# One 128-byte pad and one moved sum in a layer-norm, attention and Mish kernel

## The chip, the core and the metric

The kernel runs on one core of a Trainium2 chip. The core has TensorE for matrix products (PE in the profile, with its weight loads listed apart as PEld), VectorE (DVE), ScalarE (ACT) and GpSimd (POOL) for elementwise work, and SyncE (SP), which here issues all the DMAs. The metric is the device time of one execution in microseconds. Three executions of the kernel before took 1108.43, 1108.59 and 1108.93 us; their median is 1108.59 us.

## What is computed

All data are float32: x is 2048 x 576, and the result is the sum of x, a sliding attention and a two-layer Mish network, both on the layer-normed x. Cut to what matters:

```python
xn = layernorm(x)                                   # over the 576 columns, no scale or shift
qkv = xn @ wqkv                                     # 32 heads of 18 columns
# each position looks at itself and 7 earlier ones, 2 apart; positions before the start are masked
attn = softmax(q . k[pos - 2 * (0..7)] * 18 ** -0.5)
A = (attn-weighted sum of v) @ wo
h = xn @ w1 + b1                                    # 4608 columns
B = (h * tanh(softplus(h))) @ w2                    # Mish, then back to 576 columns
out = x + A + B
```

## The kernel before, in words

**Tiles and halves.** The 2048 tokens are worked in two halves (`hf` 0 and 1) of 1024, each half in two groups of 512 (`TB`). For each group the normed, transposed x is one tile `xt`, with a high part (rounded to the matmul format `F32R`) and a low part (the remainder), since every product is done as three products of high and low parts. The 4608 hidden columns are 18 blocks `q` of 256 (`NP`). Each block runs two steps: `m1_part` (line 738) makes the hidden activations, parts 0 to 5, and `m2_pair`, `m2_cols` or `p_item` multiply them with `w2`. Both steps use Strassen-like sums of quarters (`S` of x, `t` of the weights, `S1` to `S4` of activations), so that seven products do the work of eight.

**Weights of a block.** Block `i` of `w1` becomes four tiles: `wa`, `wc`, `t0` and `t1`. `wc` is the third block of the diff's title: 128 partitions x 2 (high, low) x 384 floats. Function `home` (line 204) gives a tile's tag and number of buffers, and `new` (line 217) allocates it. Tiles of one tag share its buffers and take them in turn, and a buffer is as large as the largest tile of the tag. Tag `wc` has 2 buffers. It also holds some weights of the first stage (`wq`, 2 x 432 floats, 3456 bytes in a partition), so that its two buffers are 3456 bytes each. All other large tiles follow or precede them in one pool. In the first half a block's tiles are made from raw loads, and kept in DRAM; in the second half they are fetched from there. The order of blocks in the second half is 1 to 17 and then 0 (`Q1`, line 33).

A product of `m1_part` has the weights as the stationary operand (128 columns at a time) and `xt` or `S` as the moving one. `wc` is used in part 3 (two matmuls of line 686) and part 5 (six of line 680 and two of line 686), ten matmuls of 512 columns for a block and half.

**The items of the second half.** In the second half, blocks 0 to 7 in the order of that half are taken two at a time (`e` = 0 to 3) into seven products each, `p_item(e, k)` (line 860), in the order `ORD`. An item runs four groups of six matmuls (line 872), each into a PSUM bank of tag `out`, of which there are four, and each followed by one addition into an SBUF accumulator: on DVE at line 878, or for some items a copy on ACT at line 876. So the next item's matmuls need the four additions of the item before. An item's left operand is an activation or a sum of activations: `u_sum` (line 807) makes the sum in place, `u_high` (line 817) its high part on ACT, `u_low` (line 822) its low part on DVE or POOL. Activations come from `mish` (line 716): ACT copies an intermediate product out of PSUM (line 714), DVE adds the next product to it (line 725), and ACT applies Mish (line 726).

**The order of work.** The order is written by hand. `plan` is a list of slots, one for each piece of matmul work; a slot has its own functions, a list of background functions (`before(i, fn)`, line 1164, appends to it), and an estimate of its time. The loop at line 1566 issues, for each slot: what the last slot left as `soon`, the background functions, what was `held` (the run of `mish` from the slot before), the slot's own functions, and then `tail`. Every engine runs its instructions in that order. Attention is cut into steps that are placed as background (`attention`, line 512): POOL multiplies (lines 539 and 577), DVE reduces (lines 544 and 583). For a few slots, among them that of item (0, 4), the set `behind_adds` (line 1495) has the pending reduction issued from `tail`, behind the slot's additions.

The moved sum is `u_sum(0, 6, 1)`: `S4` = `A12` - `S2` of the second block of pair 0, 128 x 512 floats, on DVE. Its slot is two items ahead, that of item (0, 4); before, it is a background function there, ahead of the item's four additions in DVE's order. The same sum for the first block, `u_sum(0, 6, 0)`, is on POOL and stays.

Of the kernel before, what the change touches and what calls it, by code (L numbers as in the profile page):

```python
# [9 lines left out]
F32R = mybir.dt.float32r  # L10
# [7 lines left out]
P = 128  # L18
# [21 lines left out]
def block_kernel(ctx: ExitStack, tc: tile.TileContext, x, wq, wo, w1, b1, w2, mask, out):  # L40
# [4 lines left out]
    sb = ctx.enter_context(tc.tile_pool(name="sb", bufs=2))  # L45
# [158 lines left out]
    def home(kind, i):  # L204
        if kind == "wq":
            g, k = divmod(i, 5)
            tag, bufs = (("wb", 3) if k < 3 else ("wc", 2)) if g % 2 == 0 else (("a0", 3) if k < 3 else ("a1", 2))
            return tag, bufs, 432
        if kind == "wa":
            return f"wa{(i + 1) % 2}", 1, 5 * P  # L210
        if kind == "wc":
            return "wc", 2, 3 * P
        if kind == "w2":
            return "w2", 4, D
        return "wb", 3, 4 * P

    def new(kind, hf, i):
        tag, bufs, width = home(kind, i)
        return sb.tile([P, 2, width], F32R, tag=tag, bufs=bufs, name=f"{kind}_{hf}_{i}")

    def load(kind, i):
# [20 lines left out]
    def make(kind, i):  # L242
        load({"wa": "w1", "wc": "w1", "t0": "w1", "t1": "w1"}.get(kind, kind), i)
        width = home(kind, i)[2]
        if kind == "wa":
            src = loaded["w1", i][0]
        elif kind == "wc":
            src = loaded["w1", i][1][:, 2 * P:5 * P]
        elif kind in ("t0", "t1"):
            src = sums[i][int(kind[1])]  # L250
        else:
            src = loaded[kind, i][:, 0:width]
        t = done[kind, 0, i] = new(kind, 0, i)
        nc.scalar.copy(t[:, 0, :], src)
        low[kind, i] = lambda: nc.vector.tensor_tensor(out=t[:, 1, :], in0=src, in1=t[:, 0, :].bitcast(F32),
                                                       op=ALU.subtract)
# [18 lines left out]
    def fetch(kind, i):  # L275
        w = i
        if kind == "w2":
            w = 2 * Q1[i // 2] + i % 2
        elif kind != "wq":
            w = Q1[i]  # L280
        t = done[kind, 1, i] = new(kind, 1, w)
        nc.sync.dma_start(t.rearrange("p h c -> p (h c)").bitcast(F32), kept[kind, w])
# [509 lines left out]
    def rslotof(q, x):  # L792
        k = q, int(x[1]) - 1, int(x[2]) - 1
        assert owner[where[k]] == k, (k, owner[where[k]])
        return rawact[k]

    def u_src(q, name):
        x = SLOT.get(name, name)
        assert held_.get((q, x)) == name, (q, name, held_.get((q, x)))
        return rslotof(q, x)  # L800
# [6 lines left out]
    def u_sum(e, k, qq):  # L807
        name, q = LEFT[ORD[k]], 2 * e + qq
        eng = nc.gpsimd if (name, qq) in (("S1", 1), ("S4", 0)) else nc.vector
        x, y, op = dict(S3=("A11", "A21", ALU.subtract), S2=("A22", "S3", ALU.subtract), S1=("A11", "S2", ALU.add),  # L810
                        S4=("A12", "S2", ALU.subtract)).get(name, (None,) * 3)
        if x:
            t = rslotof(q, SLOT[name])
            eng.tensor_tensor(out=t, in0=u_src(q, x), in1=u_src(q, y), op=op)
            held_[q, SLOT[name]] = name
# [21 lines left out]
    def p_fetch(e, k):  # L837
        name = RIGHT[ORD[k]]
        t = pw[e, k] = sb.tile([P, 2, 2, HC], F32R, tag="w2", bufs=4, name=f"pw_{e}_{k}")
        nc.sync.dma_start(t.bitcast(F32), kept[name, e])  # L840
# [314 lines left out]
    plan = []  # L1155
# [8 lines left out]
    def before(i, fn):  # L1164
        plan[max(i, 0)][1].append(fn)
# [24 lines left out]
    def first_cast(k, eng):  # L1190
        t = done["wq", 0, k] = new("wq", 0, k)
        nc.scalar.copy(t[:, 0, :], rq0[k])
        return lambda: eng.tensor_tensor(out=t[:, 1, :], in0=rq0[k], in1=t[:, 0, :].bitcast(F32),
                                         op=ALU.subtract)
# [161 lines left out]
    def spot(hf, q, i):  # L1356
        return at["s", hf, q, i]

    for q in range(NP):
        if q == 0:  # L1360
            i = at["q", 0, 3, 1, 0]
            ps_ = dict(raw=i - 3, sums=i - 1, wa=i, wc=i + 1, t0=i + 2, t1=i + 4)
        elif q == 1:
            i = at["q", 0, 3, 0, 0]
# [16 lines left out]
    for q in range(1, 2 * OC + 1):  # L1381
        i = spot(0, q, (3,2)[q > 1])
# [5 lines left out]
    i = spot(0, NP - 1, 0)  # L1388
# [5 lines left out]
    i = at["q", 1, 0, 1, 1]  # L1394
# [4 lines left out]
    i = spot(0, 9, 4)  # L1399
    for k in range(2):  # L1400
        for n, steps in enumerate((
# [4 lines left out]
            for kind, name in steps:  # L1406
                f = dict(l=z_load, s=z_sum, h=z_high, o=z_low, k=z_keep)[kind]
                d = 30 + 2 * n + (n >= 14) if k else 2 * n if n < 10 else (19, 20, 22, 23, 25, 26, 27)[n - 10]
                before(i + d, lambda f=f, name=name, k=k: f(name, k))
    for q in range(NP):  # L1410
        if q == 0:
            i = at["z", JB - 1, 0]
            ps_ = dict(wa=i - 7, t0=i - 6, t1=i - 5, wc=i - 4)
        elif q == 1:
            i = spot(1, 0, 0)
# [9 lines left out]
    for g, (e, k, s) in enumerate(items):  # L1425
        lead = items[g - 3][2] if g >= 3 else spot(1, 0, 5) + 2 * g
        before(lead + 1, lambda e=e, k=k: p_fetch(e, k))
        for qq in range(2):
            ds = {(0, 0): (-6, -5, -5), (0, 1): (-2, -1, -1), (1, 0): (0, -4, -2), (1, 1): (0, -2, -2), (2, 0): (0, -3, -2), (2, 1): (0, -3, -2), (3, 0): (-4, -3, -2), (3, 1): (-4, -2, -1), (4, 0): (0, -3, -3), (4, 1): (0, -3, -2), (5, 0): (-1, -3, -3), (5, 1): (0, -3, -2), (6, 0): (-4, -3, -1), (6, 1): (-4, -3, -2)}[k, qq]
            if e in (1, OC - 1) and (k, qq) == (0, 0):  # L1430
                ds = (-5, -4, -4)
            if e == 0 and k in (3, 5):
                ds = (-3, -2, -1) if k == 3 else (1,) + ds[1:]
            for d, f in zip(ds[1:], (u_high, u_low)):
                before(s + d, lambda f=f, e=e, k=k, qq=qq: f(e, k, qq))
            s2 = items[7 * e + (0 if k == 5 else k)][2] + ds[0]
            before(s2, lambda e=e, k=k, qq=qq: u_sum(e, k, qq))
    J = 2 * OC + 1
    for b in range(NB):
        for j in range(2):  # L1440
# [8 lines left out]
    i = at["q", 0, 1, 1, 0]  # L1449
# [3 lines left out]
    i = at["q", 0, 3, 1, 0]  # L1453
# [5 lines left out]
    i = at["q", 1, 0, 1, 1]  # L1459
    for n in range(8):  # L1460
        c, k = divmod(n, 4)
# [7 lines left out]
    for n in range(0, JB, 2):  # L1469
        i = at["q", 0, 1, 0, n]  # L1470
# [4 lines left out]
    for n in range(TJ):  # L1475
        i = spot(0, 2 + n, 2)
# [3 lines left out]
    i = spot(0, NP - 2, 0)  # L1480
# [7 lines left out]
    for n, (name, pr) in enumerate((name, pr) for name in ("P4", "P5", "P2", "P3") for pr in range(2)):  # L1488
        i = items[dict(P4=0, P5=2, P3=2, P2=3)[name]][2] + pr
# [26 lines left out]
    k = marks[0] - 1  # L1516
    for n in range(steps - len(last_steps)):
        t = 6.111 * n
        k = next(k for k in range(k + 1, len(plan)) if T[k + 1] > t and ok[k])
# [16 lines left out]
    i = spot(1, *(11,3))  # L1536
# [4 lines left out]
    for n, name in enumerate(("T3", "T1", "T2", "T4", "B11", "B21", "B22", "R", "D")):  # L1541
        k = i + 10 + (2, 5, 10, 15, 20, 25, 30, 35, 40)[n]
# [5 lines left out]
    i = spot(1, NP - 1, 0)  # L1548
# [71 lines left out]
```

## Time and profile before

| what | value |
|---|---|
| executions before | 1108.43, 1108.59, 1108.93 us |
| the profiled execution's own time | 1109.51 us |
| its span, first to last instruction | 1107.7 us |
| granted clock | 0.999 |
| busy: PE, PEld | 1100.8 us (99%), 1015.3 us (92%) |
| busy: DVE, POOL, ACT | 850.6 us (77%), 791.1 us (71%), 499.1 us (45%) |
| DMA | 271.60 MB, mean 245 GB/s |

The profiled execution is 0.9 us above the median of the three, and 1.8 us of its time lie outside its span. A share of busy time is a mean over stages; a matmul's end is modelled, so the times from start to start of successive matmuls say more than their durations.

### The profile page before, as it was taken

To read this page: it belongs to the slowest core of one execution; us is meant where nothing else is said; L and a number is where in the kernel's file an instruction comes from. 1 tells how busy PE (TensorE), PEld (TensorE's weight loads), DVE (VectorE), ACT (ScalarE), POOL (GpSimd) and SP (SyncE) were. 2 spreads that over 40 slices of the span, in tenths; PEclk is the share of its full clock that TensorE was granted. 3 is DMA by queue.
4 is the path that set the end of the run, shared out by engine and by line. 5 is a ranking of instruction groups with operands and counts; after the bars stand their busy time and mean duration, and the time that the engine had idled before them with its cause. 6 is when DMAs were issued, how large, how long until landed. Compare 5 with 4: busy or idle time off the path is not lost.

```text
span 1107.7 us, 18208 instructions
## 1 busy us (share of the span) xinstructions
PE 1100.8 (99%) x6550; PEld 1015.3 (92%) x6550; DVE 850.6 (77%) x1367; ACT 499.1 (45%) x917; POOL 791.1 (71%) x639
## 2 busy tenths in 40 slices
PE   9999999999999999999999999999999999999998
PEld 8999899999999999999999888989999999999998
DVE  6368788888889888898656567777876677777786
ACT  5544655544544544545333354434433344343353
POOL 2479777776779688685789667567698976867542
PEclk9999999999999999999999999999999999999999
DMA  6899696868777768676598799656674657776674
GB/s 203 284 311 308 235 343 232 282 239 266 254 259 249 266 222 296 238 263 214 170 323 268 237 358 317 223 192 208 221 222 173 210 195 224 243 288 218 179 234 140
DMA packets 178270, 271.60 MB, mean 245 GB/s; under 512 B 53218, under 2 KB 120068, under 8 KB 178180
## 3 DMA queue, kind: packets, MB, share of 16 engines
q1 hardware_dynamic: 178180, 270.44, 72.0%
q8 instruction: 52, 0.85, 0.3%
q14 instruction: 38, 0.31, 0.1%
HBM read 160.39 MB, written 110.00 MB: 244 GB/s over the span
## 4 chain that ended last, share of the span: by engine, by line
PE 94%; DMA 2%; DVE 2%; ACT 1%; POOL 1%; issue 0%; SPq 0%; DVEq 0%; POOLq 0%
PE h L680 29%; PE po L780 21%; PE po L893 11%; PE pq L348 11%; PE po L872 6%; PE h L686 6%; PE o L1076 5%; PE z L446 4%; DMA t<-kept_t 1%; DMA accP<-in_x 1%; POOL act L732 0%; PE ta L75 0%; DMA acc<-in_x 0%; DVE st L112 0%; DVE u L826 0%
## 5 line engine op out<-in xcount | busy, mean ns | idle before, releaser
L780 PEld LDWEIGHTS po<-w,act 128*128 128x128 f32 x1728 | 236.4, 188 | 6.0 <-POOL act L732 0.4
L780 PE MATMUL po<-w,act 128*128 128x288 f32 x1728 | 240.7, 295 | 0.1
L539 POOL TENSOR_TENSOR pr<-q,kv 128x576 f32<-128x576 f32 x128 | 198.2, 1574 | 9.3 <-DMA q<-q_d 6.1
L732 POOL TENSOR_TENSOR act<-c,act 128x512 fp32r<-128x512 f32 x81 | 107.4, 1326 | 128.1 <-ACT act L731 127.3
L577 POOL TENSOR_TENSOR pv<-L,kv 128x576 f32<-128x576 f32 x128 | 178.1, 1485 | 26.3 <-DVE L L570 21.4
L784 DVE TENSOR_TENSOR acc<-po,acc 128x288 f32<-128x288 f32 x288 | 119.3, 449 | 29.7 <-PE po L780 28.9
L348 PE MATMUL pq<-wq,xt 128*128 128x432 f32 x672 | 136.3, 361 | 0.9 <-ACT xt L81 0.6
L893 PEld LDWEIGHTS po<-w,act 128*128 128x128 f32 x960 | 130.9, 188 | 2.9
L893 PE MATMUL po<-w,act 128*128 128x288 f32 x960 | 132.9, 294 | 0.0
L348 PEld LDWEIGHTS pq<-wq,xt 128*128 128x128 f32 x672 | 125.1, 188 | 7.7 <-ACT xt L81 1.3
L726 ACT ACTIVATE c<-c,b1c 128x512 f32<-128x512 f32 x81 | 58.7, 725 | 138.1 <-DVE c L725 137.8
L680 PE MATMUL h<-xt,t 128*128 128x512 f32 x432 | 110.7, 391 | 0.1
L680 PE MATMUL h<-S,t 128*128 128x512 f32 x432 | 110.5, 391 | 0.0
L583 DVE TENSOR_REDUCE og<-pv 128x144 f32<-128x1152 f32 x64 | 85.9, 1345 | 24.1 <-POOL pv L577 23.9
L680 PE MATMUL h<-xt,wa 128*128 128x512 f32 x432 | 104.1, 390 | 0.0
L714 ACT COPY c<-h 128x512 f32<-128x512 f32 x81 | 47.4, 586 | 124.1 <-PE h L686 73.1
L544 DVE TENSOR_REDUCE L<-pr 128x64 f32<-128x1152 f32 x64 | 85.8, 1342 | 20.9 <-POOL pr L539 20.8
L680 PEld LDWEIGHTS h<-xt,wa 128*128 128x128 f32 x432 | 80.9, 188 | 17.0
L872 PEld LDWEIGHTS po<-pw,u 128*128 128x128 f32 x672 | 92.1, 188 | 3.5 <-DVE accP L878 1.2
L872 PE MATMUL po<-pw,u 128*128 128x288 f32 x672 | 93.8, 295 | 0.8 <-DVE accP L878 0.8
L680 PEld LDWEIGHTS h<-xt,t 128*128 128x128 f32 x432 | 79.1, 188 | 15.1 <-DVE rt L725 0.5
L896 DVE TENSOR_TENSOR accP<-po,accP 128x288 f32<-128x288 f32 x160 | 69.0, 452 | 30.2 <-PE po L893 29.4
(228 smaller groups left out, 1854.3 us busy)
## 6 DMA issues: line engine op xcount, KB each, us to landing
kv<-kv_d SPq DMA_DIRECT2D x64, 396.0 KB, 5.2
kept_t<-t SPq DMA_DIRECT2D x36, 512.0 KB, 4.4
t<-kept_t SPq DMA_DIRECT2D x36, 512.0 KB, 6.5
rw<-in_w SPq DMA_DIRECT2D x36, 320.0 KB, 4.5
kept_wa<-wa SPq DMA_DIRECT2D x18, 640.0 KB, 4.9
kept_w<-w SPq DMA_DIRECT2D x20, 576.0 KB, 4.1
wa<-kept_wa SPq DMA_DIRECT2D x18, 640.0 KB, 5.2
w<-kept_w SPq DMA_DIRECT2D x20, 576.0 KB, 4.3
```

Of the source, the lines that this page charges most:

```text
L348: nc.tensor.matmul(pq[:, 0:432], XT[:, xi, tok], wt[wi][:, hl, 0:432], start=i == 0, stop=i == len(seq) - 1)
L539: nc.gpsimd.tensor_tensor(out=pr[:, x:x + hh], in0=q[:, j0 + x:j0 + x + hh, None, :].to_broadcast([P, hh, W, CU]), in1=win(kt, 0, CU, j0 + ...
L544: nc.vector.tensor_reduce(L[:, k, j0:j0 + hj].rearrange("p j w h -> p (j w h)"), pr.rearrange("p j w (h d) -> p (j w h) d", h=2), axis=AX, ...
L577: nc.gpsimd.tensor_tensor(out=pr[:, x:x + hj].rearrange("p j d w -> p j w d"), in0=L[:, k, x:x + hj, :, h:h + 1].to_broadcast([P, hj, W, DH]),
L583: nc.vector.tensor_reduce(og[:, c0:c0 + DH, :].rearrange("p d j -> p j d"), pr, axis=AX, op=ALU.add)
L680: nc.tensor.matmul(ph, wt[:, wl, wk * P:(wk + 1) * P], X[:, xs, :], start=first and i == 0, stop=last and i == len(seq) - 1, skip_group_ch ...
L732: nc.gpsimd.tensor_tensor(out=a[:, 1, :], in0=t, in1=a[:, 0, :].bitcast(F32), op=ALU.subtract)
L780: nc.tensor.matmul(po, acts[hf, q, b, j][:, al, tok], done["w2", hf, 2 * q + j][:, wl, c * HC:(c + 1) * HC], start=i == 0, stop=i == 5)
L784: nc.vector.tensor_tensor(out=t, in0=po, in1=t, op=ALU.add)
L872: nc.tensor.matmul(po, units[e, k, qq][:, al, tok], w[:, qq, wl, :], start=i == 0, stop=i == 5)
L893: nc.tensor.matmul(po, acts[hf, q, b, j][:, al, tok], done["w2", hf, 2 * q + j][:, wl, c * HC:(c + 1) * HC], start=i == 0, stop=i == 5)
L896: nc.vector.tensor_tensor(out=t, in0=po, in1=t, op=ALU.add)
```

## The change

There are two edits. A tile of tag `wc` made by `new` is allocated as 128 x 896 floats (3584 bytes in a partition, 14 x 256) and cut to its old shape by a view; the buffers of the tag grow from 3456 to 3584 bytes, so that the second lies 128 bytes farther on, and all tiles behind the two 256 bytes farther. And the sum `u_sum(0, 6, 1)` is appended to its slot's own functions, behind `p_item(0, 4)`, where it was a background function of the slot.

```diff
     def new(kind, hf, i):
         tag, bufs, width = home(kind, i)
+        if tag == "wc":
+            return sb.tile([P, 7 * P], F32R, tag=tag, bufs=bufs, name=f"{kind}_{hf}_{i}")[:, 0:2 * width].rearrange(
+                "p (h c) -> p h c", h=2)
         return sb.tile([P, 2, width], F32R, tag=tag, bufs=bufs, name=f"{kind}_{hf}_{i}")
...
             s2 = items[7 * e + (0 if k == 5 else k)][2] + ds[0]
-            before(s2, lambda e=e, k=k, qq=qq: u_sum(e, k, qq))
+            plan[s2][0 if (e, k, qq) == (0, 6, 1) else 1].append(lambda e=e, k=k, qq=qq: u_sum(e, k, qq))
```

## The prediction, made before the result was known

> **What bounds the kernel now.** I read the page first: the span, the busy shares and the chain of work that ended last.
>
> ```profile
> span 1107.7 us, 18208 instructions
> ...
> PE 1100.8 (99%) x6550; PEld 1015.3 (92%) x6550; DVE 850.6 (77%) x1367; ACT 499.1 (45%) x917; POOL 791.1 (71%) x639
> ...
> PE 94%; DMA 2%; DVE 2%; ACT 1%; POOL 1%; issue 0%; SPq 0%; DVEq 0%; POOLq 0%
> ```
>
> PE is busy in 1100.8 of 1107.7 us and carries 94% of the chain. So there are only two ways to gain: to take away one of PE's few waits, or to make matmuls follow each other faster. The two edits aim at one of each. The list of PE's waits comes next:
>
> ```profile
> PE warm L65 <- POOL ident masks.py:199: 1.3, 1, 1.3
> PE po L872 <- DVE accP L878: 0.8, 1, 0.8
> ```
>
> The list has five rows; the other three are single waits of 0.6 us and less for the first normed x and the first weights, in the start. After that there is one wait: an item's matmuls (L872) wait once, 0.8 us, for the additions of the item before (DVE L878). Then the costs of matmuls by group, since PE is otherwise never idle:
>
> ```profile
> L680 PE MATMUL h<-xt,t 128*128 128x512 f32 x432 | 110.7, 391 | 0.1
> ...
> L680 PE MATMUL h<-xt,wa 128*128 128x512 f32 x432 | 104.1, 390 | 0.0
> ...
> L680 PE MATMUL h<-S,wc 128*128 128x512 f32 x216 | 55.8, 393 | 0.0
> L686 PE MATMUL h<-xt,wc 128*128 128x512 f32 x144 | 45.0, 394 | 0.0
> ```
>
> All these have 512 moving columns and 128 stationary ones. With `t` or `wa` as weights the mean is 390 to 391 ns, with `wc` 393 to 394. The third block's tile is the odd one out, and the change pads its buffers.
>
> **The padding.** It adds no instruction, no wait and no DMA, and moves none in any queue, SP's included; the bytes of each load and store stay 2 x 384 floats a partition. What changes is addresses. A buffer of 3456 bytes is 13.5 x 256, so now the two buffers of the tag differ by half of 256 bytes in where they start; at 3584 bytes they agree. Tiles take the buffers in turn, so odd blocks have the second and even blocks the first, in both halves (in the second half one `R2` tile takes the first buffer ahead of block 1). If the address matters, odd and even blocks must differ. I look at the timeline of PE for the same pair of matmuls (part 3) in successive blocks 9, 10, 11 of the first half, and 13, 14, 15 of the second:
>
> ```profile
> 321.44 0.64 PE L686 MATMUL h<-xt,wc 128*128 128x512 f32 x2
> ...
> 345.59 0.62 PE L686 MATMUL h<-xt,wc 128*128 128x512 f32 x2
> ...
> 369.67 0.64 PE L686 MATMUL h<-xt,wc 128*128 128x512 f32 x2
> ...
> 906.18 0.64 PE L686 MATMUL h<-xt,wc 128*128 128x512 f32 x2
> ...
> 930.35 0.62 PE L686 MATMUL h<-xt,wc 128*128 128x512 f32 x2
> ...
> 954.44 0.64 PE L686 MATMUL h<-xt,wc 128*128 128x512 f32 x2
> ```
>
> The pair shows 0.64 us in odd blocks and 0.62 in even ones. A whole block, which holds the same matmuls each time, takes 345.59 - 321.44 = 24.15 us from an odd block's pair to the next, and 369.67 - 345.59 = 24.08 from an even one's: 0.07 more with the second buffer. In the second half it is 24.17 against 24.09, 0.08 more. For the early blocks of the second half, where items lie between, I compare block 5 with block 6, from the start of a run to the start of what follows it:
>
> ```profile
> 709.83 0.64 PE L686 MATMUL h<-xt,wc 128*128 128x512 f32 x2
> 710.32 0.97 PE L872 MATMUL po<-pw,u 128*128 128x288 f32 x6
> ...
> 718.54 1.55 PE L680 MATMUL h<-S,wc 128*128 128x512 f32 x6
> ...
> 720.40 1.78 PE L680 MATMUL h<-xt,wa 128*128 128x512 f32 x7
> ...
> 730.88 0.62 PE L686 MATMUL h<-xt,wc 128*128 128x512 f32 x2
> 731.34 0.83 PE L872 MATMUL po<-pw,u 128*128 128x288 f32 x5
> ...
> 739.56 1.53 PE L680 MATMUL h<-S,wc 128*128 128x512 f32 x6
> ...
> 741.37 1.98 PE L680 MATMUL h<-xt,wa 128*128 128x512 f32 x8
> ```
>
> Part 3's pair: 0.49 against 0.46 us. Part 5's eight (six of L680 and two of L686 behind them): 720.40 - 718.54 = 1.86 against 741.37 - 739.56 = 1.81. Together 0.08. I take 0.07 for the nine odd blocks of the first half and 0.08 for the nine of the second: 0.63 + 0.72 = 1.35, rounded to **-1.4 us** since the matmuls next to the runs show a few ns too. The rows are rounded to 0.01, which on a difference of two stretches is worth 0.02 a block, 0.4 in all: the bounds are -1.0 and -1.8. None of it needs cover: PE is the bound and takes it directly, unless a later wait eats it (a rival below).
>
> The Trainium skill speaks against this edit: "SBUF — State Buffer", section "Who interferes with whom", says that PE never waits on another engine's SBUF access, and names only VectorE's and GpSimd's shared ports as a place of contention; it knows no cost of a matmul's operand address. By that page the edit is worth 0 and the sum would be 1108.6. The trace disagrees with 24.15 against 24.08 us, and I go by the trace.
>
> **The moved sum.** Around PE's 0.8 us wait the timeline of all engines reads:
>
> ```profile
> 683.03 1.74 POOL L814 TENSOR_TENSOR ra<-ra,rm 128x512 f32<-128x512 f32 x1
> 683.55 1.77 DVE L814 TENSOR_TENSOR rm<-rm,rm 128x512 f32<-128x512 f32 x1
> ...
> 684.73 7.04 POOL L539 TENSOR_TENSOR pr<-q,kv 128x576 f32<-128x576 f32 x4
> ...
> 685.24 1.54 DVE L878 TENSOR_TENSOR accP<-po,accP 128x288 f32<-128x288 f32 x4
> 685.43 0.62 ACT L820 CAST u<-rm 128x512 fp32r<-128x512 f32 x1
> ...
> 685.74 3.47 PE L872 MATMUL po<-pw,u 128*128 128x288 f32 x24 [0.81 <-DVE accP L878]
> 685.95 0.58 ACT L714 COPY rt<-h 128x512 f32<-128x512 f32 x1
> 686.70 1.34 DVE L544 TENSOR_REDUCE L<-pr 128x64 f32<-128x1152 f32 x1
> 687.96 0.68 DVE L826 TENSOR_TENSOR u<-rm,u 128x512 fp32r<-128x512 f32 x1
> 688.56 0.68 DVE L725 TENSOR_TENSOR rt<-h,rt 128x512 f32<-128x512 f32 x1
> ...
> 689.29 1.23 PEld L680 LDWEIGHTS h<-xt,t 128*128 128x128 f32 x6 [0.32 <-DVE rt L725]
> ```
>
> The moved sum is the DVE row at 683.55, 1.77 us. Behind it stand the four additions (685.24), and PE waits 0.81 us for them. With the sum behind them the additions start at 683.55 and end at 685.09, the first bank is free at about 684.0, and PE goes on without the wait, at 685.74 - 0.81 = 684.93. So far the edit gains 0.81.
>
> What is late next? The item's 24 matmuls would end 0.81 earlier, at 688.40 instead of 689.21. The next matmul (689.29, part 4) accumulates into the bank that DVE's addition L725 reads, and starts 0.05 after that addition's end at 689.24; the weight-load row names it as releaser. So the wait moves there, unless that addition is earlier as well. DVE works without a pause from 683.55 to 689.24, and the move only permutes its order, so the addition is earlier only if the sum gets shorter. Its price here:
>
> ```profile
> L814 DVE TENSOR_TENSOR rm<-rt,rm x6: 649/687/1777, 655.2 to 790.1; 128x512 f32<-128x512 f32 x6
> ...
> L539 POOL TENSOR_TENSOR pr<-q,kv x128: 1415/1440/2022, 57.4 to 1017.5; 128x576 f32<-128x576 f32 x128
> ```
>
> Such a sum takes 0.65 to 0.69 us alone and 1.78 at worst. At 683.55 it was long because POOL's sum (683.03, ended 684.77) ran ahead of it: 684.77 + 0.6 is its end. In its new place it would be issued at about 685.05, and POOL has begun the first of four multiplications at 684.73, 1.44 alone, so until 686.17. If the sum waits for that again it ends at 686.17 + 0.68 = 686.85, and the reduction L544 begins at about 686.77 where it began at 686.70. Then the addition L725 ends as now, within 0.1, PE's next matmul starts as now, and the edit is worth **0**. If it doesn't wait, it ends at 685.7, all behind it comes 1.0 earlier, and PE gains 0.81 and the 0.08 that it now has between item and part 4: -0.89. On the other side: ACT's high part of the sum (685.43) moves with the sum to about 686.9, and the copy L714 (685.95), which the addition L725 reads, queues behind it to 688.0, with 0.5 us to spare to 688.56; and DVE's low part at 687.96, now 0.68, needs the high part by then. If it came later than POOL's next multiplication it would take 1.7, and PE would lose 1.0 to 1.2. Bounds: -0.89 and +1.2; I take 0, by the pair of rows 683.03 and 683.55, the nearest case of a sum issued behind a POOL instruction under way.
>
> What the Trainium skill says in the section cited above agrees with those two rows and would fix the choice: a VectorE instruction with two SBUF inputs is held for the whole of a GpSimd instruction that reads SBUF and came first. By that rule the edit is worth 0; were there no such lock it would be worth -0.89.
>
> **Sum.** Against the profiled execution's own time: 1109.51 - 1.4 + 0 = 1108.1 us. The median shown, 1108.59, lies 0.9 lower than that execution, so the forecast for the median is 1108.59 - 1.4 = **1107.2 us**. A measurement of this kernel can tell about 0.2% from no change, which is 2.2 us, so the lines lie at 1106.4 and 1110.8.
>
> **The rivals.** *Both gains arrive.* The sum runs between POOL's multiplications instead of behind one, DVE is 1 us ahead, and PE never waits: 1108.59 - 1.4 - 0.89 = 1106.3 us, beyond the line by a hair. For it: POOL's start at 684.73 may shift by some tenths, and the sum's row has 0.65 as its lowest. Against: POOL's row shows four multiplications in 7.04 us, with hardly a pause between, so the sum can hardly be issued outside one.
>
> *The padding is worth nothing*, because a block's excess is due to something else that alternates (`wa` has two homes too), or because what PE gains it then waits for: 1108.6. Against: the excess sits in the rows with `wc`.
>
> *The shift costs more than the pad brings*, the rival on the slower side. All tiles behind the two buffers move by 256 bytes: `w2`, the activations, `S`, one `xt`, `wa`. If matmuls care for 256 bytes as they do for 128, each product of activations and `w2` changes: 1728 at L780, 960 at L893 and 672 at L872.
>
> ```profile
> L780 PE MATMUL po<-w,act 128*128 128x288 f32 x1728 | 240.7, 295 | 0.1
> ...
> L893 PE MATMUL po<-w,act 128*128 128x288 f32 x960 | 132.9, 294 | 0.0
> ...
> L872 PE MATMUL po<-pw,u 128*128 128x288 f32 x672 | 93.8, 295 | 0.8 <-DVE accP L878 0.8
> ```
>
> The groups with `t` and `wa` above differ by 1 ns, which bounds what different homes do: at 1 to 2 ns over 3360 matmuls it costs 3.4 to 6.7 us, and the time is 1110.6 to 1113.9, say 1112. It ends slower by over 0.2% from 1.1 ns a matmul on ((2.2 + 1.4) / 3360). Against: in the program's list of addresses the homes of `t` and `wa` lie an odd multiple of 256 bytes apart, and their groups agree to that 1 ns; half of 256 is what `wc` shows.
>
> **How the numbers follow.** The forecast (pad -1.4, sum 0) has 0.48, both gains 0.30, no gain 0.12, the shift 0.10. So faster by over 0.2%: 0.30; within: 0.48 + 0.12 = 0.60; slower: 0.10. The range reaches from both gains with the upper bound of the pad partly taken in (1106.0) to no gain (1108.7), and leaves out the shift and the ends of the bounds.
>
> **What would show it.** Right: the two L686 stretches of blocks 9 and 10 equal at 24.08; all `wc` pairs at 0.62; the additions of item (0, 4) ahead of the sum; PE's wait on accP L878 gone, and one of about 0.8 to 0.9 on rt L725 in its place. The second gain has come if that wait is missing and the sum took 0.7. Wrong: odd blocks still longer by 0.07; means of L780 or L893 off by a ns or more; any new wait of PE over 0.3 us elsewhere.

## The result, and the profile after

| series | kernel before, median (lowest to highest, executions) | changed kernel | ratio, 95% interval |
|---|---|---|---|
| first | 1108.74 us (1108.19 to 1115.92, 18) | 1106.66 us (1106.27 to 1107.44, 18) | 0.9968 [0.9955, 0.9981] |
| second | 1109.09 (1108.36 to 1110.31, 21) | 1106.95 (1106.14 to 1107.61, 11) | 0.9981 [0.9972, 0.9990] |
| third | 1108.86 (1108.01 to 1116.08, 29) | 1107.59 (1106.41 to 1107.94, 12) | 0.9972 [0.9956, 0.9989] |

By medians the change is worth -2.1, -2.1 and -1.3 us. The ratio follows the means (1106.68 and 1110.37 in the first series), and the kernel before has single executions of 1113.8 to 1116.1 us (5 of 18 in the first series, none of 21 in the second, 8 of 29 in the third), of which the changed kernel had none. Without those five, the means of the first series stand at 0.9982, near the second series with none (0.9981); without its eight, the third stands at 0.9987. So about 2.0 us (0.18%) of the first series' 3.7 us (0.32%) is the ordinary gain, and 1.7 us is that tail; it has a section of its own below.

The page of the changed kernel (execution 1106.93 us, granted clock 1.000), then the list of PE's waits, then the groups of matmuls (busy us, mean ns | idle before). Lines stand three higher: L680 is now L683, L686 is L689, L872 is L875.

```profile
span 1105.1 us, 18208 instructions
...
PE 1098.0 (99%) x6550; PEld 1014.0 (92%) x6550; DVE 849.1 (77%) x1367; ACT 499.1 (45%) x917; POOL 790.8 (72%) x639
```

```profile
...
PE ta L75 <- ACT xn L180: 0.9, 2, 0.5
PE h L683 <- DVE rt L728: 0.4, 1, 0.4
```

```profile
L783 PE MATMUL po<-w,act 128*128 128x288 f32 x1728 | 240.6, 295 | 0.1
...
L896 PE MATMUL po<-w,act 128*128 128x288 f32 x960 | 132.9, 295 | 0.0
...
L683 PE MATMUL h<-xt,wa 128*128 128x512 f32 x432 | 103.9, 389 | 0.0
...
L683 PE MATMUL h<-S,wc 128*128 128x512 f32 x216 | 55.4, 392 | 0.0
L689 PE MATMUL h<-xt,wc 128*128 128x512 f32 x144 | 44.4, 389 | 0.0
```

PE's busy time fell by 2.8 us, the span by 2.6. The two `wc` groups went from 393 and 394 ns to 392 and 389, `xt,wa` from 390 to 389; the products of activations (L783, L896) stand within 1 ns. PE's wait on accP is gone, and one on rt is there.

The timeline of PE for the pairs of blocks 9, 10, 11 in the first half and 13, 14, 15 in the second:

```profile
321.19 0.61 PE L689 MATMUL h<-xt,wc 128*128 128x512 f32 x2
...
345.27 0.61 PE L689 MATMUL h<-xt,wc 128*128 128x512 f32 x2
...
369.35 0.62 PE L689 MATMUL h<-xt,wc 128*128 128x512 f32 x2
...
903.80 0.62 PE L689 MATMUL h<-xt,wc 128*128 128x512 f32 x2
...
927.88 0.62 PE L689 MATMUL h<-xt,wc 128*128 128x512 f32 x2
...
951.96 0.62 PE L689 MATMUL h<-xt,wc 128*128 128x512 f32 x2
```

Each of these blocks takes 24.08 us, odd or even, in both halves. The odd blocks' 24.15 and 24.17 us of before are gone.

The timeline of all engines around item (0, 4):

```profile
681.99 1.53 DVE L881 TENSOR_TENSOR accP<-po,accP 128x288 f32<-128x288 f32 x4
...
683.18 6.96 POOL L542 TENSOR_TENSOR pr<-q,kv 128x576 f32<-128x576 f32 x4
...
683.45 1.71 DVE L817 TENSOR_TENSOR rm<-rm,rm 128x512 f32<-128x512 f32 x1
...
683.92 3.33 PE L875 MATMUL po<-pw,u 128*128 128x288 f32 x24
...
685.08 1.34 DVE L547 TENSOR_REDUCE L<-pr 128x64 f32<-128x1152 f32 x1
...
686.94 0.68 DVE L728 TENSOR_TENSOR rt<-h,rt 128x512 f32<-128x512 f32 x1
...
687.68 1.63 PE L683 MATMUL h<-xt,t 128*128 128x512 f32 x6 [0.42 <-DVE rt L728]
```

The additions (681.99) now run ahead of the sum (683.45), and the item's matmuls start without a wait. The sum was issued 0.27 us behind the start of POOL's first multiplication and took 1.71 us again. So the addition L728 came no earlier relative to PE, and PE waits 0.42 us for it.

### The profile page after: what moved, and what is told of

Its sections match the earlier page's. It is cut to its first block, busy times and chain, and to the rows that moved or that the text cites. A ratio compares the mean times of both kernels' runs of the same rounds, so it can differ in the third digit from the quotient of the medians.

```text
span 1105.1 us, 18208 instructions
## 1 busy us (share of the span) xinstructions
PE 1098.0 (99%) x6550; PEld 1014.0 (92%) x6550; DVE 849.1 (77%) x1367; ACT 499.1 (45%) x917; POOL 790.8 (72%) x639
## 4 chain that ended last, share of the span: by engine, by line
PE 92%; DMA 3%; DVE 2%; ACT 1%; SPq 1%; POOL 1%; issue 1%; DVEq 0%; POOLq 0%
PE h L683 28%; PE po L783 21%; PE po L896 11%; PE pq L351 11%; PE po L875 6%; PE h L689 5%; PE o L1079 5%; PE z L449 3%; DMA accP<-in_x 1%; DMA t<-kept_t 1%; DMA kv<-kv_d 1%; SPq L615 1%; DMA pw<-kept_T 0%; POOL act L735 0%; DMA acc<-in_x 0%
## 5 line engine op out<-in xcount | busy, mean ns | idle before, releaser
L783 PEld LDWEIGHTS po<-w,act 128*128 128x128 f32 x1728 | 236.3, 188 | 5.8 <-POOL act L735 0.4
L783 PE MATMUL po<-w,act 128*128 128x288 f32 x1728 | 240.6, 295 | 0.1
L896 PEld LDWEIGHTS po<-w,act 128*128 128x128 f32 x960 | 130.9, 188 | 2.8
L896 PE MATMUL po<-w,act 128*128 128x288 f32 x960 | 132.9, 295 | 0.0
L683 PE MATMUL h<-xt,t 128*128 128x512 f32 x432 | 110.5, 391 | 0.4 <-DVE rt L728 0.4
L683 PE MATMUL h<-S,t 128*128 128x512 f32 x432 | 110.4, 391 | 0.0
L683 PE MATMUL h<-xt,wa 128*128 128x512 f32 x432 | 103.9, 389 | 0.0
L683 PEld LDWEIGHTS h<-xt,wa 128*128 128x128 f32 x432 | 81.0, 188 | 16.6
L875 PEld LDWEIGHTS po<-pw,u 128*128 128x128 f32 x672 | 91.9, 188 | 2.2
L875 PE MATMUL po<-pw,u 128*128 128x288 f32 x672 | 93.4, 294 | 0.0
L683 PEld LDWEIGHTS h<-xt,t 128*128 128x128 f32 x432 | 79.1, 188 | 15.3 <-DVE rt L728 0.9
```

Of the source, the lines that this page charges most:

```text
L683: nc.tensor.matmul(ph, wt[:, wl, wk * P:(wk + 1) * P], X[:, xs, :], start=first and i == 0, stop=last and i == len(seq) - 1, skip_group_ch ...
L783: nc.tensor.matmul(po, acts[hf, q, b, j][:, al, tok], done["w2", hf, 2 * q + j][:, wl, c * HC:(c + 1) * HC], start=i == 0, stop=i == 5)
L875: nc.tensor.matmul(po, units[e, k, qq][:, al, tok], w[:, qq, wl, :], start=i == 0, stop=i == 5)
L896: nc.tensor.matmul(po, acts[hf, q, b, j][:, al, tok], done["w2", hf, 2 * q + j][:, wl, c * HC:(c + 1) * HC], start=i == 0, stop=i == 5)
```

## The experiments

Theory 1: a matmul's pace depends on where its operand starts modulo 256 bytes; the pad brings the gain alone, and the moved sum only moves a wait. The rivals: the moved sum brings part of the gain; or the gain comes from the changed homes of the other tiles.

### One edit at a time

The pad alone (`e1_pad_only`):

```diff
+        if tag == "wc":
+            return sb.tile([P, 7 * P], F32R, ...)[:, 0:2 * width].rearrange("p (h c) -> p h c", h=2)
```

> Only the padding of the third block's buffers; the sum stays ahead of the additions. Theory 1 (the start of the weights modulo 256 bytes sets a matmul's cost, and the moved sum is worth half a microsecond or less): -1.4 us against the kernel before, all stretches from pair to pair equal at 24.08 us, and PE still waits once, 0.4 to 0.8 us, for the additions of item (0, 4). Rival (the padding is small and the moved sum, or what it sets right in DVE's order, brings most of the gain of the whole change): under 0.7 us of gain.

Measured: 1107.01 us (1106.45 to 1107.54, 11 executions) against 1108.83 before, ratio 0.998 [0.997, 0.999]. The gain is 1.8 us by medians, somewhat more than the 1.4 expected.

The moved sum alone (`e2_move_only`):

```diff
-            before(s2, lambda e=e, k=k, qq=qq: u_sum(e, k, qq))
+            plan[s2][0 if (e, k, qq) == (0, 6, 1) else 1].append(lambda e=e, k=k, qq=qq: u_sum(e, k, qq))
```

> Only the moved sum, with the old buffers. Theory 1: -0.4 us (0 to -0.8) against the kernel before; PE's wait on the additions gone and a wait of 0.4 to 0.9 us on the addition L725 in its place; odd blocks still 0.07 us longer than even ones. Rival (the sum brings most): -1.2 us or more, with no wait of PE near item (0, 5).

Measured: 1108.89 us (1108.0 to 1114.01, 12) against 1108.83, ratio 1.0 [0.9988, 1.0012]. In its trace PE's wait on accP is gone and 0.39 us on rt L725 stands in its place. The pad carries the gain; the move alone brings none that can be seen, where 0.4 us was expected.

The pad alone and the whole change again, side by side (`e11_pad_again`, `e12_after_again`, no further edit):

> The padding alone again, in one call with the changed kernel, for the worth of the moved sum once the buffers are padded. Theory 1: the two agree within 0.4 us.

> The changed kernel again, beside the padding alone: the moved sum is worth 0 to 0.4 us on top of the padding.

Measured: 1107.39 us (1106.63 to 1108.96, 12), ratio 0.9972 [0.9954, 0.999], and 1107.59 us, ratio 0.9972 [0.9956, 0.9989]. The move on top of the pad costs 0.2 us side by side. Over all series the medians are 1107.31 (23 executions of the pad alone) and 1106.86 (41 of the whole change), which makes it a gain of 0.45; but medians of the kernel before differ by 0.35 between series. The move can't be told from 0.

The traces say why. The wait that it was to take is not firm. PE waits on accP for 0.81 and 0.88 us in two traces of the kernel before, but with the pad alone for 0.24 in one trace and not at all in the other (0.11 and 0.09 then come at the next part). The pad isn't what takes it away: with the old buffers it is 0.02 us in `e3_scan` and 0 in `e14_low_pool`, and with padded ones 0.37 in `e13_pad_bad_again` (these runs come below). With the move, the wait on rt is 0.42, 0.75 and 0.66 in three traces.

The kernel before and the whole change, one trace each beside other runs (`e5_null`, `e8_after`, no edit):

> The kernel before, unchanged, for a second profile of it. In the first one PE waits 0.81 us for the additions of item (0, 4), while the padding alone shows 0.24 us there and the moved sum alone is worth nothing. Theory 1: the first profile was an execution with late loads of x, and an ordinary one of the kernel before has a wait of 0 to 0.4 us there, so that the moved sum has next to nothing to take away. Rival: the wait is 0.8 us again, and the padding takes it away.

> The changed kernel again, on the chip of its neighbours in this call. Theory 1: -1.8 to -2.2 us against the kernel before, as for the padding alone, within 0.4 us of it.

Measured: 1109.74 us, with the 0.88 us wait on accP, so that the 0 to 0.4 us expected for an ordinary execution was missed; and 1106.95 us (1106.14 to 1107.61, 11), ratio 0.9981 [0.9972, 0.9990], with 0.75 us on rt.

### Is it the start modulo 256?

Both buffers padded, but the tile 128 bytes farther in, where the second buffer of the kernel before starts: 192 modulo 256 in both, in place of 64 (`e4_pad_bad`, and again as `e13_pad_bad_again`):

```diff
-            return sb.tile([P, 7 * P], ...)[:, 0:2 * width]...
+            return sb.tile([P, 7 * P], ...)[:, 32:32 + 2 * width]...
```

> The padded buffers, but the tile begins 128 bytes inside its buffer, so that both buffers have the slow residue 192 instead of the fast one 64; the sum stays ahead of the additions. The suspected cost of the kernel before is doubled: theory 1 expects +1.4 us against the kernel before (+2.8 against the padding alone), with odd and even blocks alike at about 24.15 us from pair to pair. Rival (two buffers that agree is what counts, not where they begin): the same gain as the padding alone, -1.4 us. The first stage's weights in these buffers shift too.

Measured: 1110.23 us (1109.85 to 1111.39, 11), ratio 1.0009 [0.9999, 1.0019] against the kernel before, 3.2 us more than the pad alone beside it. Its groups:

```profile
L683 PE MATMUL h<-S,wc 128*128 128x512 f32 x216 | 56.2, 395 | 0.0
...
L689 PE MATMUL h<-xt,wc 128*128 128x512 f32 x144 | 45.7, 399 | 0.0
```

The products with `wc` are now slow in every block (395 and 399 ns against 392 and 389), and blocks of the kind timed above, odd and even, take 24.15 us in the first half and 24.18 in the second. The homes of all other tiles are those of the pad alone. The size of the buffers and the shift of the other tiles are ruled out as the cause; the start is it.

The start moved by 32 bytes from block to block inside the old buffers (`e3_scan`):

```diff
+        if kind == "wc":
+            off = 8 * (i % 8)
+            return sb.tile([P, 864], F32R, ...)[:, off:off + 768].rearrange("p (h c) -> p h c", h=2)
```

> The kernel before, with the old buffers of 3456 bytes, but the third block's tile of block i begins 32 * (i mod 8) bytes inside its buffer, so that its weights begin at all eight multiples of 32 modulo 256 in turn. Read from the trace are the stretches of the ten matmuls with these weights, block by block. Theory 1 (the start modulo 256 counts): blocks with i mod 8 = 4, which now begin at the residue that the second buffer had, 192, take the long stretches (pair 0.48 us, eight 1.85 to 1.87), although they are even and lie in the first buffer; the other odd blocks do not all stay long. Rival (something else that alternates with the blocks' parity): all odd blocks stay long and all even ones short, whatever the offset. Whether a residue is faster than 64 (pair under 0.45 us) is open.

Measured: 1109.92 us in one execution. Its timeline of PE, at the pairs of blocks 8, 9 and 12, which start at 64, 224 and 192, each with the row behind it (L690 and L784 are L686 and L780 of before):

```profile
297.86 0.62 PE L690 MATMUL h<-xt,wc 128*128 128x512 f32 x2
298.31 3.34 PE L784 MATMUL po<-w,act 128*128 128x288 f32 x24
...
321.95 0.62 PE L690 MATMUL h<-xt,wc 128*128 128x512 f32 x2
322.41 3.34 PE L784 MATMUL po<-w,act 128*128 128x288 f32 x24
...
394.47 0.64 PE L690 MATMUL h<-xt,wc 128*128 128x512 f32 x2
394.95 3.35 PE L784 MATMUL po<-w,act 128*128 128x288 f32 x24
```

From start to start the pair takes 0.45, 0.46 and 0.48 us. Block 12 has the first buffer, the fast one of before, and is now the slowest: it isn't the buffer. Over the blocks of the trace it is 453 or 454 ns at 64, 460 to 468 at 0, 32, 96, 128, 160 and 224, and 481 at 192 (but for one block of 633, which takes 614 in the kernel before too). The eight of part 5 take 1818 to 1824 ns at 64 in five blocks of six (1838 in the first block) and 1837 to 1873 elsewhere, but for two of 1960 and 1972 where the halves meet.

### Is 64 good, or agreement?

By the program's list of addresses all large tiles of the changed kernel start at 64 modulo 256, `xt` and `S` among them. So either the start of `wc` itself counts, or its agreement with the moving operand. First, the scan again with the third `S` tile moved to 192 (`e6_scan_moving`):

```diff
+            if k == 2:
+                Ss[hf, k] = sb.tile([P, 4 * TB + 64], ...)[:, 32:32 + 4 * TB].rearrange("p (k t) -> p k t", k=4)
```

> As the scan of starts (the third block's tile begins 32 * (i mod 8) bytes inside the old buffers), and besides the third S tile, which is the moving operand of part 5's six matmuls with these weights and of no other of part 3 or 5, begins 128 bytes farther, at 192 modulo 256 instead of 64. Theory A (weights and moving operand must begin at the same place modulo 256): the six are now fast, 226 to 227 ns from start to start, where the weights begin at 192 (i mod 8 = 4) and slow where they begin at 64 (i mod 8 = 0 and block 8, 16); part 3's pair, whose moving operand stays at 64, is as in the first scan, 453 ns at 64 and 481 at 192. Theory B (the weights' own start counts): six and pair as in the first scan, both fast at 64 alone.

Measured: 1110.93 us in one execution. The pair, whose moving operand `xt` stays at 64, is as in the scan: 453 ns at 64, 481 at 192. The eight, which hold the six with the moved `S`, take 1843 to 1866 ns at 64 and 1840 to 1848 at 192, 1834 to 1875 in all (but for two of 1932 and 1969 where the halves meet): nowhere the fast 1818 to 1824. In block 8, at 64, the six went from 1370 to 1386 ns; in block 12, at 192, from 1396 to 1389. So the start of the moving operand counts too, and both theories of the expectation fall as they stand: neither the start of `wc` alone nor its agreement with its own moving operand gives the fast pace.

Then 32 bytes put ahead of all tiles of the changed kernel, so that all start at 96 (`e10_all_96`):

```diff
+    fill = const.tile([P, 8], F32, name="fill")
+    nc.vector.memset(fill, 0.0)
```

> The changed kernel with a filler of 32 bytes ahead of the pool, so that all large tiles begin at 96 modulo 256 instead of 64: all operands still begin at one residue, but another. Theory C (64 itself is the good residue; 96 costs the third block's ten matmuls 6 to 40 ns a stretch in the scan): all matmuls of 512 columns slow by 4 to 6 ns, 1650 of them, +7 us or more, and those of 288 columns by some ns more, up to +20 us in all. Theory D (what counts is that all operands agree): within 1 us of the changed kernel.

Measured: 1106.34 us in one execution.

```profile
L683 PE MATMUL h<-S,wc 128*128 128x512 f32 x216 | 55.3, 392 | 0.0
...
L689 PE MATMUL h<-xt,wc 128*128 128x512 f32 x144 | 44.3, 389 | 0.0
```

At 96 throughout, the groups are as fast as at 64. In the scan 96 among tiles at 64 was slow (460 ns a pair), so 64 is nothing special. The reading that fits the three runs is that tiles used near each other should start alike. It is a reading and not shown: the second half of the columns of a `w2` tile lies 1152 bytes (4.5 x 256) behind the first and so starts 128 bytes off in every kernel here. How one matmul hangs on the operands of its neighbours, as the moved `S` suggests, stays open.

### The wait that is left, and the widths of products

The low part of the same activations (`u_low(0, 6, 1)`) moved one slot later, so that the addition L728 comes ahead of it (`e7_late_low`):

```diff
+            if (e, k, qq) == (0, 6, 1):
+                ds = (-4, -3, -1)
```

> The changed kernel, and the low part of the moved sum (u_low of item (0, 6), second block) one slot later, so that DVE's addition L725 (now L728) of item (0, 5)'s slot stands ahead of it. If that addition is what PE now waits for, the wait of 0.4 us goes: -0.3 to -0.5 us against the changed kernel, which runs in the same call. Rival (the low part becomes late for item (0, 6)): a wait of 0.3 us or more at that item, no gain or a loss.

Measured: 1107.36 us (1106.54 to 1107.55, 11), ratio 0.9982 [0.9974, 0.9991], against 1106.95 of the changed kernel beside it. Its timeline of PE:

```profile
690.57 0.66 PE L875 MATMUL po<-pw,u 128*128 128x288 f32 x3 [0.43 <-DVE u L829]
```

The wait on rt is 0.43 us, where the changed kernel had 0.42, 0.75 and 0.66, and a new one of 0.43 stands at item (0, 6), which needs the low part. So the rival of the expectation came: moved one slot later, the low part is late, and it takes 1.91 us there (0.68 in the changed kernel).

The 576 columns of the first half's `w2` products cut into 320 and 256 in place of twice 288, so that each second part starts at a multiple of 256 bytes (`e9_split`):

```diff
-            for c in range(2):
+            for c, (c0, c1) in enumerate(((0, 320), (320, D))):
```

> The changed kernel, and in the first half the products of activations with w2 cut their 576 columns into 320 and 256 instead of 288 and 288, so that the second cut's moving columns begin at 64 modulo 256 bytes, as all fast operands do, and not at 192. In the trace before, such a group of six matmuls takes 798.6 ns with the second cut and 789.6 with the first, and there are 144 of each in the first half. Theory (the moving operand's start counts as the weights' does): 9 ns for each of 144 groups, -1.3 us against the changed kernel; sum of a pair of groups 1579 instead of 1588 ns. Rival (the 9 ns belong to the place in the order, or 256 columns are bound by the weight load): no gain, or a loss of up to 1 us.

Measured: 1109.42 us (1109.08 to 1111.23, 12), 1.8 us over the changed kernel beside it; ratio to the kernel before 0.9985 [0.9966, 1.0003]. From its timeline:

```profile
322.70 3.35 PE L783 MATMUL po<-w,act 128*128 128x320 f32 x24
325.90 1.55 PE L683 MATMUL h<-xt,t 128*128 128x512 f32 x6
327.28 0.61 PE L689 MATMUL h<-xt,wa 128*128 128x512 f32 x2
```

The 24 products take 3.20 us against 3.18 in the changed kernel, and the six behind them 1.38 against 1.37. The first half has 72 such runs of 24, so 0.02 us on each makes about 1.4 of the 1.8 us. Both expectations missed: aligned starts of the second parts brought no gain, and the loss is more than the 1 us allowed. The widths changed along with the starts, so the run doesn't tell what a start alone would do.

### The long executions

The one long execution that was profiled is that of the moved sum alone (1114.01 us). Its timeline of all engines:

```profile
808.30 1.36 POOL L814 TENSOR_TENSOR ra<-ra,rm 128x512 f32<-128x512 f32 x1
...
808.52 7.18 DVE L826 TENSOR_TENSOR u<-ra_r,u 128x512 fp32r<-128x512 f32 x1 [0.20 <-ACT u L820]
...
809.54 2.89 POOL L539 TENSOR_TENSOR pr<-q,kv 128x576 f32<-128x576 f32 x2
...
812.32 2.83 POOL L881 TENSOR_TENSOR accP<-accP,accP 128x576 f32<-128x576 f32 x2
...
816.23 1.54 DVE L878 TENSOR_TENSOR accP<-po,accP 128x288 f32<-128x288 f32 x4
...
816.77 4.87 PE L872 MATMUL po<-pw,u 128*128 128x288 f32 x24 [3.87 <-issue]
```

and the busy time of its engines in two stretches (the columns end with the granted clock, the DMA share and GB/s):

```profile
810.00:812.80 2.80, 2.80 (x22) 2.67 (x20) 2.80 (x1) 0.32 (x1) 2.80 (x3) 1.00 0.33 137
816.70:820.00 3.30, 3.23 (x13) 3.26 (x14) 3.27 (x6) 0.92 (x2) 0.00 (x0) 0.50 0.14 52
```

DVE's addition was issued 0.22 us behind POOL's and was held through five POOL instructions, until 815.70. DVE's four additions came 816.23, and PE, which needs them, stood for 3.87 us. Then the granted clock was 0.50, and matmuls followed each other at 240 ns for some 13 of them, where 127 to 139 is usual: 1.4 us more. Together 5.3, about the execution's distance of 5.1 from its kernel's median of 1108.89. This agrees with the Trainium skill, "TensorE: Matmul & The Clock Gate", "Part 1: The HAM clock gate", by which an idle window of about 3.4 us halves the clock for about as long.

The theory that this addition, issued so close behind POOL's, makes the long executions was put to two runs. One was the kernel with both starts at 192 again, where the addition is issued 0.18 to 0.26 us behind POOL's (in the changed kernel it is 0.98); the other the kernel before with that addition on POOL (`e14_low_pool`):

```diff
-        eng = nc.gpsimd if (name, qq) in (...) else nc.vector
+        eng = nc.gpsimd if (name, qq) in (...) or (e, name, qq) == (3, "S2", 1) else nc.vector
```

> Both buffers of the third weight block start at 192 modulo 256 bytes, as in the kernel of the run that measured 1110.2 us. Theory L (the executions of 1113.8 us and more that the kernel before shows, 14 of 97 so far, come from the VectorE addition u<-ra_r,u that is issued about 0.2 us behind the start of GpSimd's ra<-ra,rm and is then held for 7 us): here that addition was issued 0.26 us behind that start in the profiled run, as in the kernels with long executions, so some of about 11 executions may lie at 1114 to 1117 us; none in 11 was seen before. Rival M (long executions go with buffers of 2304 bytes whatever the times of issue): none above 1112 us. The median stays at 1110.2, 1.4 us over the kernel before, with either.

> The kernel before with one addition of the low activations (third item group, second slice, second quarter: the u<-ra_r,u that was held for 7.18 us) issued on GpSimd in place of VectorE. Theory L: no execution above 1112 us, while the kernel before beside it shows some at 1113.8 to 1116 (about one in seven so far); the median within 0.5 us of the kernel before. Rival M (the long executions have another cause): long executions here at about the rate of the kernel before. If the kernel before shows none beside it, the run tells nothing on this.

Measured: 1110.31 us (1110.08 to 1111.28, 11), ratio 1.0014 [1.0005, 1.0022], none long; and 1108.74 us (1108.27 to 1112.4, 11), ratio 1.0004 [0.9995, 1.0013], against 1108.82 before, which had none in 21 beside them. The one execution of 1112.4 has a clock of 0.998, as the long ones have (0.996 to 0.998), though that addition isn't on DVE there. So the theory isn't borne out: the close issue came without long executions in 22 (11 of each run with both starts at 192), and one of 1112.4 came without the instruction. It isn't ruled out either, since the kernel before beside the last two runs had no long execution. The counts stand: the kernel before had 14 executions over 1113 us in 118, 13 of them in two series (5 of 18 and 8 of 29); the kernels with padded buffers had none over 1111.4 in 110, 18 and 37 of them in these two series. One padded execution of 1111.23 us (`e9_split`) has a clock of 0.998 too. Whether padded buffers avoid the long executions, and why, is open. (The old buffers have 3456 bytes, not the 2304 that an expectation names.)

## Why the prediction was right or wrong

**The pad's mechanism was right.** All blocks at 24.08, all pairs at 0.61 to 0.62, the pad alone with the whole gain, and both starts at 192 with the opposite sign. The page of the Trainium skill weighed in the prediction ("SBUF — State Buffer", "Who interferes with whom"), by which PE never waits for others, would have made it 0; the runs give 1107.01 against 1108.83 us and, with the place inside the padded buffer as the only difference, 1110.23 against 1107.01. The gain is no wait of the kind that the page speaks of; it has no price for where an operand starts.

**The pad's size failed at the term "0.08 for the nine of the second", 0.72 us, which measured about 1.4 over the second half.** It took the late blocks' excess for the early ones too, and backed it with the pair and the eight of block 5 against block 6. Block 5 in the changed kernel, from PE's timeline:

```profile
708.18 0.61 PE L689 MATMUL h<-xt,wc 128*128 128x512 f32 x2
708.64 3.33 PE L875 MATMUL po<-pw,u 128*128 128x288 f32 x24
711.80 1.53 PE L683 MATMUL h<-xt,t 128*128 128x512 f32 x6
...
716.79 1.53 PE L683 MATMUL h<-S,wc 128*128 128x512 f32 x6
...
718.61 2.88 PE L683 MATMUL h<-xt,wa 128*128 128x512 f32 x12
721.33 0.62 PE L689 MATMUL h<-xt,wa 128*128 128x512 f32 x2
...
729.04 0.61 PE L689 MATMUL h<-xt,wc 128*128 128x512 f32 x2
```

and the rows of the kernel before that the prediction left out of its run:

```profile
710.32 3.38 PE L872 MATMUL po<-pw,u 128*128 128x288 f32 x24
713.53 1.55 PE L680 MATMUL h<-xt,t 128*128 128x512 f32 x6
...
720.40 2.93 PE L680 MATMUL h<-xt,wa 128*128 128x512 f32 x12
723.17 0.62 PE L686 MATMUL h<-xt,wa 128*128 128x512 f32 x2
```

The block took 730.88 - 709.83 = 21.05 and takes 729.04 - 708.18 = 20.86: 0.19 less, where 0.08 was counted. The pair gives 0.03 of it, the eight 0.04. Most of the rest is in matmuls that don't touch `wc`: the 24 of the item behind the pair take 713.53 - 710.32 = 3.21 against 3.16, the twelve `xt,wa` behind the eight 2.77 against 2.72. The shift of the other tiles is not the cause, since with the same homes and only the start of `wc` at 192 (`e4_pad_bad`) they are slow again, 3.21 and 2.77:

```profile
711.37 3.38 PE L875 MATMUL po<-pw,u 128*128 128x288 f32 x24
714.58 1.55 PE L683 MATMUL h<-xt,t 128*128 128x512 f32 x6
...
721.45 2.93 PE L683 MATMUL h<-xt,wa 128*128 128x512 f32 x12
724.22 0.62 PE L689 MATMUL h<-xt,wa 128*128 128x512 f32 x2
```

So a slow pace, once set, is carried on by matmuls that follow. A slow start of `wc` isn't all that can set it: behind the fast pair of block 6 the 24 take 3.21 in both kernels (734.55 - 731.34 and 732.70 - 729.49), and what sets it there is open. Blocks 3, 7 and 9 show the same as block 5 (0.19 to 0.21), the late blocks 11 to 17 0.09. In the first half the twelve `xt,wa` behind the eight take 2.72 in both kernels, and 0.067 a block is right. The comparison of blocks 5 and 6 was cut off at the end of the run, where the excess goes on.

PE's pace in whole traces says the same. From the first matmul's start to the last one's, less all idle time ahead of matmuls:

| buffers | traces | us |
|---|---|---|
| as before | before, `e5_null`, `e14_low_pool` | 1100.5, 1099.7, 1099.1 |
| padded, at 64 | `e1`, `e11`, after, `e8`, `e12` | 1097.1, 1097.8, 1097.7, 1098.2, 1097.7 |
| padded, at 192 | `e4`, `e13` | 1101.3, 1100.6 |

The means are 1099.8, 1097.7 and 1100.9: the pad is worth -2.1 in matmuls alone, the wrong start +1.1. Traces with the same buffers scatter by 0.7 to 1.4, but nearly all of that lies ahead of the first block's pair, where they take 103.3 to 104.9 whatever the buffers. Cut at the pairs of the first blocks of each half and of the last block, the same sums are:

| buffers | first half | second half | behind |
|---|---|---|---|
| as before | 523.50 to 523.57 | 391.28 to 391.53 | 80.59 to 80.60 |
| padded, at 64 | 522.96 to 523.02 | 389.87 to 390.21 | 80.59 to 80.61 |
| padded, at 192 | 524.18 | 392.27 to 392.34 | 80.69 to 80.72 |

By the means the pad is worth -0.56 in the first half, where the prediction had 0.63, and -1.41 in the second, where it had 0.72; together -2.0, and the wrong start is worth +1.6. The medians of the pad alone gave -1.8 and -1.5, those of the wrong start +1.4 and +1.5. Idle time ahead of matmuls is 2.4 to 3.4 us before and 2.3 to 3.1 in the changed kernel.

**The moved sum: right at 0, and by the working given.** The sum was issued behind POOL's multiplication and held, and the wait went to rt, 0.39 to 0.75 us instead of the 0.8 to 0.9 named. What the prediction didn't see is that the 0.81 it started from was no constant: traces with the same order on DVE have 0 to 0.88.

**The rivals.** *Both gains arrive* names nearly the measured time (1106.3) for a reason that failed: the sum did not take 0.7 and PE did not go on without a wait. *The padding is worth nothing* fell with the pad alone (1107.01 against 1108.83), *the shift costs more* with L783 and L896 within 1 ns of before.

**A term left out: the tail.** The forecast's time was 0.5 us too high, inside its range. But the change it forecast was 1.4 us, and the first series gives 2.1 by medians and 3.7 by means. About 0.6 of the difference is the pad's term above; the other 1.7 is the long executions of the kernel before, which count in the means and for which the sum has no term. None of the three times it was worked out from was long. The chances set most on "within 0.2%", with the line at 2.2 us; the gain lies just inside that line by medians and beyond it by means.

## What to carry to other kernels

When a kernel's bound is the succession of matmuls, compare the same matmuls in successive turns of a rotating buffer; an alternation may come from where the buffers start. Padding the buffer to a multiple of 256 bytes, so that its turns start alike, cost nothing here but the bytes. Carry such a comparison past the end of the run that touches the tile, over the whole period. A sum that only changes places in a full engine's order can move a wait and not remove it: ask what comes last next before counting the wait as gain.

## What the runs showed of the hardware that was not expected

- A pair of 512-column float32 matmuls takes 453 ns where all large tiles start alike modulo 256 bytes (64, or 96 in `e10_all_96`), 460 to 468 at other starts of its weights, 481 with a difference of 128 bytes. The matmuls that follow can carry the slower pace on, 0.05 us over 24 that don't read the tile.
- A VectorE addition with two SBUF inputs was held for 7.18 us, through five GpSimd instructions in a row. The Trainium skill, "SBUF — State Buffer", "Who interferes with whom", has such an instruction wait for the GpSimd instruction that came first; here it waited for four more that came later.
- PE's stop of 3.87 us was followed by 3.3 us at a granted clock of 0.50, so that a wait in the middle of a kernel cost 1.4 us more than its length.
